# Linear attention gated with a shift-MLP block: DMA transposes, x^T phi(k) in place of v, and the attention output summed into the last MLP product

## The chip, the cores and the metric

The kernel runs on one core of a Trainium2 chip. The metric is the device time of one execution, in microseconds (us). Every number below is a median of several executions, unless one execution is named. The profile is taken of one execution. Its span is from the first to the last instruction. Executions can fall into a slower state, and only runs in the fast state are compared.

TensorE appears in the profile as PE (matmuls) and PEld (weight loads, which overlap matmuls), VectorE as DVE, ScalarE as ACT, GpSimd as POOL, SyncE's queue as SPq. PSUM is the memory that matmuls write to; SBUF is the one that holds their inputs. The granted clock is the share of TensorE's full clock that the throttle let through.

## The reference, cut to what matters

The input x is 2048 tokens by 640 channels. Branch A is linear attention with 32 heads of 20 channels. Branch B is a layernorm, a product with `w1`, a gelu, a shift of token positions, a product with `w2`, then a second layernorm and an MLP of inner width 1728. A gate g per token mixes the two.

```python
g = sigmoid((x * gate_w).sum(-1, keepdims=True))

# branch A; phi(t) = where(t > 0, t + 1, exp(t)) + 1e-6
q, k, v = split(x @ wqkv)                    # 32 heads of 20
kv  = einsum("bhsd,bhse->bhde", phi(k), v)
z   = einsum("bhsd->bhd", phi(k))
num = einsum("bhqd,bhde->bhqe", phi(q), kv)
den = einsum("bhqd,bhd->bhq", phi(q), z)[..., None] + 1e-6
a   = concat_heads(num / den) @ wo

# branch B
h  = gelu(layernorm(x) @ w1)
hs = concat(four quarters of h, shifted by 1, -1, 2, -2 tokens) @ w2
x1 = x + hs
b  = x1 + gelu(layernorm(x1) @ w3) @ w4      # w3: 640 x 1728

out = g * a + (1 - g) * b
```

Two facts let the algebra be rearranged. First, `phi(k)^T v = (x^T phi(k))^T Wv`, so v need never be computed per token. Second, `kv` and `wo` can be multiplied once, to a 640x640 matrix M, so that `a = (phi(q)/den) @ M`. With `g/(1-g) = e^y`, where y is the gate's logit, the output is `(1-g) * (x1 + h2 + (phi(q) * e^y/den) @ M)`, and the last two terms can be accumulated in one PSUM tile.

## The kernel before

The products of this program contract over the partition axis of their inputs, so each activation is needed with channels on partitions. This kernel makes these layouts on TensorE: five 128x128 transposes into PSUM, then one copy by ScalarE.

```python
def transpose_to(dst, src_tok):
    trp = tr_pool["p"].tile([P, DC, P], BF16, name="trp")
    for dc in range(DC):                                   # DC = 5
        nc.tensor.transpose(trp[:, dc, :], src_tok[:, dc * P:(dc + 1) * P], ident[:])
    nc.scalar.copy(dst, trp[:])
```

It is used four times for each of the 16 chunks of 128 tokens: for x, layernorm(x), the attention output o and layernorm(x1). That makes 320 transposes. Outputs of 640 columns are computed in pieces of 512 and 128 columns. The inner width of 1728 is padded with zeros to 14 groups of 128 rows.

```python
if F % P:                                                  # F = 1728, P = 128
    nc.gpsimd.memset(w3_sb[:, :, F:FC * P], 0.0)
    nc.gpsimd.memset(w4_sb[F % P:P, nfull, :], 0.0)
...
# branch A of one chunk, cut
#   pn = phi(q) @ [kv | z];  o_tok = pn * (1/den)
transpose_to(oT[:], o_tok[:])
for (n0, n1) in ((0, 512), (512, D)):
    for dc in range(DC):
        nc.tensor.matmul(pa[:, n0:n1], lhsT=oT[:, dc, :], rhs=wo_sb[:, dc, n0:n1], ...)
nc.scalar.activation(ga[:], pa[:], ACT.Copy, scale=g_all[:, c:c + 1])
...
# last product of one chunk: 28 matmuls
for (n0, n1) in ((0, 512), (512, D)):
    for fc in range(FC):                                   # FC = 14, all of 128 rows
        nc.tensor.matmul(pf[:, n0:n1], lhsT=h2T[:, fc, cc * P:(cc + 1) * P], rhs=w4_sb[:, fc, n0:n1],
                         start=(fc == 0), stop=(fc == FC - 1))
```

Of the kernel before, what the change touches and what calls it, by code (L numbers as in the profile page):

```python
# [8 lines left out]
ACT = mybir.ActivationFunctionType  # L9
# [8 lines left out]
def kernel(  # L18
# [23 lines left out]
    GW = 120  # L42
    NG = 6
    gsz = [GW] * 5 + [D - 5 * GW]
    FC = (F + P - 1) // P
    fsz = [P] * (F // P) + ([F % P] if F % P else [])
    EPS = 1e-5
    CG = D // 4
    shifts = [1, -1, 2, -2]

    x2 = A_x.rearrange("b s d -> (b s) d")
    out2 = out.rearrange("b s d -> (b s) d")

    const = ctx.enter_context(tc.tile_pool(name="const", bufs=1))
    small = ctx.enter_context(tc.tile_pool(name="small", bufs=4))

    ident = const.tile([P, P], BF16)
    make_identity(nc, ident[:])
    hlo = [(P * j) // Dh for j in range(DC)]
    hhi = [(P * j + P - 1) // Dh for j in range(DC)]  # L60
    nhj = [hhi[j] - hlo[j] + 1 for j in range(DC)]
    NHM = max(nhj)
    koff = [0, 160, 320, 512, 672]
    HB0 = 24
    bmask = const.tile([P, DC, NHM * Dh], F32)
    nc.gpsimd.memset(bmask[:], 1.0)
    for j in range(DC):
        off = P * j - Dh * hlo[j]
        nc.gpsimd.affine_select(out=bmask[:, j, :], in_=bmask[:, j, :], compare_op=ALU.is_ge, fill=0.0,
                                base=off, pattern=[[-Dh, NHM], [0, Dh]], channel_multiplier=1)  # L70
        nc.gpsimd.affine_select(out=bmask[:, j, :], in_=bmask[:, j, :], compare_op=ALU.is_ge, fill=0.0,
                                base=Dh - 1 - off, pattern=[[Dh, NHM], [0, Dh]], channel_multiplier=-1)
    ones_col = const.tile([P, 1], BF16)
    nc.vector.memset(ones_col[:], 1.0)

    wo_sb = const.tile([P, DC, D], BF16)
    w2_sb = const.tile([P, DC, D], BF16)
    w3_sb = const.tile([P, DC, FC * P], BF16)
    w4_sb = const.tile([P, FC, D], BF16)
    hsT = const.tile([P, DC, S + 4], BF16)  # L80
    pqT = const.tile([P, DC, S], BF16)
    y_all = const.tile([P, NCH], F32)
    g_all = const.tile([P, NCH], F32)
    omg_all = const.tile([P, NCH], F32)
    kv_ext = const.tile([P, DC, NHM * (Dh + 1)], BF16)
    zc = const.tile([P, DC], F32)

    mid = ctx.enter_context(tc.tile_pool(name="mid", bufs=1))
    w1_sb = mid.tile([P, DC, D], BF16)
    lnxT = mid.tile([P, DC, S], BF16)  # L90
    s1 = ExitStack()
    st1 = s1.enter_context(tc.tile_pool(name="st1", bufs=1))
    wkvg = st1.tile([P, DC, 2 * D + 2], BF16)
    wq_sb = st1.tile([P, DC, D], BF16)
    xT = st1.tile([P, DC, S], BF16)
    x_sb = st1.tile([P, NCH, D], BF16)
    w1p = s1.enter_context(tc.tile_pool(name="w1p", bufs=2))
    ps_tr1 = s1.enter_context(tc.tile_pool(name="ps_tr1", bufs=2, space=PSUM))
    ps_kv = s1.enter_context(tc.tile_pool(name="ps_kv", bufs=1, space=PSUM))
    ps_mm = s1.enter_context(tc.tile_pool(name="ps_mm", bufs=4, space=PSUM))  # L100

    wqkv_v = A_wqkv.rearrange("(c p) f -> p c f", p=P)
    w1_v = B_w1.rearrange("(c p) f -> p c f", p=P)
    nfull = F // P
# [5 lines left out]
    load_x(0, 1)  # L110
    dq.dma_start(wkvg[:, :, 0:512], wqkv_v[:, :, D:D + 512])
    load_x(1, 2)
    dq.dma_start(wkvg[:, :, 512:1024], wqkv_v[:, :, D + 512:D + 1024])
    dq.dma_start(wkvg[:, :, 1024:2 * D], wqkv_v[:, :, D + 1024:3 * D])
    dq.dma_start(wkvg[:, :, 2 * D:2 * D + 1], gate_w.rearrange("(c p o) -> p c o", p=P, o=1))
    load_x(2, 4)
    dq.dma_start(wq_sb[:, :, 0:D], wqkv_v[:, :, 0:D])
    load_x(4, 8)
    for g in range(4):
        dq.dma_start(w1_sb[:, :, P * g:P * (g + 1)], w1_v[:, :, CG * g:CG * g + P])  # L120
        dq.dma_start(w1_sb[:, :, 4 * P + 32 * g:4 * P + 32 * (g + 1)], w1_v[:, :, CG * g + P:CG * (g + 1)])
    load_x(8, 12)
    load_x(12, 16)
    for g in range(4):
        dq.dma_start(w2_sb[:, g, :], B_w2[CG * g:CG * g + P, :])
        dq.dma_start(w2_sb[32 * g:32 * (g + 1), 4, :], B_w2[CG * g + P:CG * (g + 1), :])
    dq.dma_start(wo_sb[:], A_wo.rearrange("(c p) f -> p c f", p=P))
    dq.dma_start(w3_sb[:, :, 0:F], B_w3.rearrange("(c p) f -> p c f", p=P))
    dq.dma_start(w4_sb[:, 0:nfull, :], B_w4[0:nfull * P, :].rearrange("(c p) f -> p c f", p=P))
    if F % P:  # L130
        dq.dma_start(w4_sb[0:F % P, nfull, :], B_w4[nfull * P:F, :])

    if F % P:
        nc.gpsimd.memset(w3_sb[:, :, F:FC * P], 0.0)
        nc.gpsimd.memset(w4_sb[F % P:P, nfull, :], 0.0)
    nc.vector.memset(hsT[:, :, 0:4], 0.0)
    nc.vector.memset(hsT[:, :, S:S + 4], 0.0)
    kvacc = ps_kv.tile([P, 1024], F32)
    nc.vector.memset(kvacc[:], 0.0)
# [13 lines left out]
    def ln_stats(mv_ap, src_ap):  # L153
        st = small.tile([P, 2, 6], F32, name="bnst")
        nc.vector.bn_stats(st[:, 0, :], src_ap[:, 0:D // 2])
        nc.vector.bn_stats(st[:, 1, :], src_ap[:, D // 2:D])
        nc.vector.bn_aggr(mv_ap, st[:])

    tr_pool = {"p": ps_tr1}

    def transpose_to(dst, src_tok):
        trp = tr_pool["p"].tile([P, DC, P], BF16, name="trp")
        for dc in range(DC):
            nc.tensor.transpose(trp[:, dc, :], src_tok[:, dc * P:(dc + 1) * P], ident[:])  # L164
        nc.scalar.copy(dst, trp[:])  # L165

    def phi_from_psum(dst_bf16, src_ps, npart, ncols, tagp):
        e = w1p.tile([P, 640], F32, name="e_" + tagp)
        nc.scalar.activation(e[:npart, :ncols], src_ps, ACT.Exp)  # L169
        nc.vector.tensor_scalar(e[:npart, :ncols], e[:npart, :ncols], 1.0, 1e-6, op0=ALU.min, op1=ALU.add)  # L170
        nc.vector.scalar_tensor_tensor(dst_bf16, src_ps, 0.0, e[:npart, :ncols], op0=ALU.max, op1=ALU.add)  # L171

    xT_done = set()

    def ensure_xT(c):
        if c not in xT_done:
            xT_done.add(c)
            transpose_to(xT[:, :, c * P:(c + 1) * P], x_sb[:, c, :])

    def stage1_chunks(t, ln1_tile=None):  # L180
        if ln1_tile is not None:
            stage1_ln1_stats(ln1_tile)
        for cc in range(CPT):
            c = t * CPT + cc
            cs = slice(c * P, (c + 1) * P)
            xc = x_sb[:, c, :]
            ensure_xT(c)
            if c + 1 < NCH:
                ensure_xT(c + 1)
            pk_sb = w1p.tile([P, D], BF16, name="pk_sb")  # L190
            v_sb = w1p.tile([P, D], BF16, name="v_sb")
            col_blocks = [(0, 512), (512, 1024), (1024, 2 * D + 1)]
            for (c0, c1) in col_blocks:
                pt = ps_mm.tile([P, 512], F32, name="mm")
                for dc in range(DC):
                    nc.tensor.matmul(pt[:, 0:c1 - c0], lhsT=xT[:, dc, cs], rhs=wkvg[:, dc, c0:c1],  # L196
                                     start=(dc == 0), stop=(dc == DC - 1))
                if c0 < D:
                    k1 = min(c1, D)
                    phi_from_psum(pk_sb[:, c0:k1], pt[:, 0:k1 - c0], P, k1 - c0, "k")  # L200
                if c1 > D:
                    v0 = max(c0, D)
                    v1 = min(c1, 2 * D)
                    nc.scalar.copy(v_sb[:, v0 - D:v1 - D], pt[:, v0 - c0:v1 - c0])  # L204
                if c1 > 2 * D:
                    nc.vector.tensor_copy(y_all[:, c:c + 1], pt[:, 2 * D - c0:2 * D - c0 + 1])
            for j in range(DC):
                w_ = Dh * nhj[j]
                v0 = Dh * hlo[j]
                nc.tensor.matmul(kvacc[:, koff[j]:koff[j] + w_], lhsT=pk_sb[:, j * P:(j + 1) * P], rhs=v_sb[:, v0:v0 + w_],  # L210
                                 start=False, stop=(c == NCH - 1), skip_group_check=True)
                nc.tensor.matmul(kvacc[:, koff[j] + w_:koff[j] + w_ + 1], lhsT=pk_sb[:, j * P:(j + 1) * P], rhs=ones_col[:],
                                 start=False, stop=(c == NCH - 1), skip_group_check=True)
            if ln1_tile is not None:
                stage1_ln1_chunk(ln1_tile * CPT + cc)

    ln1_state = {}

    def stage1_ln1_stats(t):
        mv = const.tile([P, CPT, 2], F32, name=f"mv1_{t}")  # L220
        for cc in range(CPT):
            ln_stats(mv[:, cc, :], x_sb[:, t * CPT + cc, :])
        veps = small.tile([P, CPT], F32, name="veps1")
# [14 lines left out]
    def stage1_ln1(t):  # L238
        stage1_ln1_stats(t)
        for cc in range(CPT):  # L240
            stage1_ln1_chunk(t * CPT + cc)
# [262 lines left out]
```

## Time and profile before

The time was 322.37 us (322.27 to 322.65 in four runs). The page's first part gives busy time, share of the span and number of instructions by engine, and its fourth part gives the shares of the chain of work that ended last.

```profile
PE 296.6 (92%) x2064; PEld 160.3 (50%) x2064; DVE 163.7 (51%) x507; ACT 155.7 (48%) x271; POOL 5.5 (2%) x19
...
PE 69%; DVE 13%; ACT 12%; DMA 2%; issue 2%; SPq 1%; ACTq 0%
```

TensorE is busy for 92% of the span and no other engine for more than 51%. So this is a kernel whose time is read from TensorE, and the useful question is how much of the 296.6 us is work and how much is waiting hidden between matmuls. For that I count columns: a matmul streams its columns at 2.4 per ns, plus about 2.5 ns. The traces show this rate: matmuls of 512 and 128 columns follow one another every 216 and 56 ns. The page's groups of instructions show what the work is (line, engine, operation, output<-inputs, shape, count, then busy us and mean ns of one, then idle time before them and its releaser).

```profile
L446 PE MATMUL tokw<-w_sb,h2T 128*128 128x512 bf16 (+1 forms) x392 | 57.5, 299 | 0.6 <-DVE oc L449 0.6
...
L165 ACT COPY xT<-trp 128x640 bf16<-128x640 bf16 x16 | 11.3, 703 | 4.4 <-PE trp L164 4.4
```

The mean of 299 ns in the first of the groups is the length that the profile gives to one matmul, not the distance between two, and it mixes two shapes. Distances between starts are what add up.

| Before, TensorE | columns | us at the stream rate |
|---|---|---|
| k and v projections, gate column | 102,480 | |
| q, w1, w2, o@wo (51,200 each) | 204,800 | |
| w3 and w4 (143,360 each) | 286,720 | |
| phi(k)^T v with z, and phi(q) [kv, z] | about 23,700 | |
| 320 transposes | 40,960 | 17 of the total |
| total | about 658,700 | 279.6 |
| lost: first 20 us / 20 to 100 us / 100 to 175 us / rest | | 14 / 6 / 10 to 12 / the rest of 42 |

The loss between 100 and 175 us is read from the windows: window, its length, then busy us of PE, PEld, DVE, ACT and POOL with instruction counts, the granted clock, the DMA share, GB/s.

```profile
100.00:120.00 20.00, 17.56 (x123) 9.51 (x122) 6.86 (x15) 14.06 (x24) 0.00 (x0) 1.00 0.06 17
...
160.00:180.00 20.00, 16.30 (x125) 8.84 (x123) 15.71 (x49) 6.08 (x8) 0.00 (x0) 1.00 0.11 33
```

### The profile page before, as it was taken

What the parts mean: (1) busy time and instruction counts of PE and PEld (TensorE: products, weight loads), DVE (VectorE), ACT (ScalarE), POOL (GpSimd) and SP (SyncE); (2) the same over time, 40 slices, a digit from 0 to 9 for tenths busy, and PEclk for the clock granted to TensorE, in tenths of its full rate; (3) what the DMA queues carried; (4) which work ended last, traced back from release to release, by engine and by line L of the source; (5) the groups of instructions that cost most, each with busy time, mean ns of one, the idle gap of its engine ahead of it and who ended that gap; (6) DMA issues with size and microseconds to landing.
All of it is one profiled execution on the core that took longest, in us unless ns stands there. A gap on an engine that the chain in (4) does not pass through costs nothing.

```text
span 321.5 us, 5167 instructions
## 1 busy us (share of the span) xinstructions
PE 296.6 (92%) x2064; PEld 160.3 (50%) x2064; DVE 163.7 (51%) x507; ACT 155.7 (48%) x271; POOL 5.5 (2%) x19
## 2 busy tenths in 40 slices
PE   3589999999999799899979899999999999999995
PEld 1246645656544354445435555454555544545453
DVE  4679977585793266423577535960226780111022
ACT  3245656767657936965424442378013368113400
POOL 6000000000000000000000000000000000000000
PEclk9959999999999999999999999999999999999999
DMA  7998930000000011000010011100011000010011
GB/s 237 287 281 270 371 108 1 3 0 2 0 2 0 0 43 43 20 2 0 2 41 20 22 43 41 42 22 0 22 41 43 0 0 3 20 43 21 0 43 41
DMA packets 19144, 17.54 MB, mean 55 GB/s; under 512 B 6768, under 2 KB 18480, under 8 KB 19120
## 3 DMA queue, kind: packets, MB, share of 16 engines
q1 hardware_dynamic: 19120, 17.21, 17.7%
q8 instruction: 16, 0.26, 0.4%
q14 instruction: 8, 0.07, 0.1%
HBM read 14.58 MB, written 2.62 MB: 54 GB/s over the span
## 4 chain that ended last, share of the span: by engine, by line
PE 69%; DVE 13%; ACT 12%; DMA 2%; issue 2%; SPq 1%; ACTq 0%
PE tokw L446 15%; PE mm L196 9%; PE mm L248 6%; PE tokw L330 6%; PE tokc L396 6%; PE trp L164 3%; PE mm L258 3%; PE tokc L446 2%; PE kvacc L210 2%; ACT hsT L266 2%; DMA x_sb<-in_A_x_dram 2%; ACT v_sb L204 2%; PE tokc L373 2%; ACT lnx1T L165 1%; DVE pk_sb L171 1%
## 5 line engine op out<-in xcount | busy, mean ns | idle before, releaser
L446 PE MATMUL tokw<-w_sb,h2T 128*128 128x512 bf16 (+1 forms) x392 | 57.5, 299 | 0.6 <-DVE oc L449 0.6
L196 PE MATMUL mm<-wkvg,xT 128*128 128x512 bf16 (+1 forms) x240 | 51.9, 361 | 3.5 <-DVE pk_sb L171 3.5
L446 PEld LDWEIGHTS <-h2T 128*128 128x128 bf16 x448 | 35.2, 98 | 28.0 <-issue 1.7
L449 DVE SCALAR_TENSOR_TENSOR oc<-tokw,omg_all,ga 128x640 bf16<-128x640 f32 x14 | 12.4, 884 | 71.8 <-PE tokw L446 71.8
L432 PEld LDWEIGHTS <-w_sb 128*128 128x128 bf16 x280 | 25.8, 97 | 25.2 <-issue 1.2
L196 PEld LDWEIGHTS <-xT 128*128 128x128 bf16 x240 | 22.8, 101 | 19.0 <-issue 4.1
L330 PE MATMUL tokw<-w_sb,hsT 128*128 128x512 bf16 (+1 forms) x160 | 27.4, 299 | 4.3 <-ACT hsT L266 1.9
L399 ACT ACTIVATE ga<-tokc,g_all 128x640 f32<-128x640 f32 x16 | 12.7, 791 | 29.4 <-PE tokc L396 29.4
L396 PE MATMUL tokc<-wo_sb,oT 128*128 128x512 bf16 (+1 forms) x160 | 24.7, 300 | 1.4 <-ACT oT L165 1.1
L165 ACT COPY oT<-trp 128x640 bf16<-128x640 bf16 x16 | 11.1, 691 | 28.3 <-PE trp L164 24.6
L248 PE MATMUL mm<-xT,wq_sb 128*128 128x512 bf16 x100 | 22.5, 379 | 0.0
L169 ACT ACTIVATE e_k<-mm 128x512 f32<-128x512 f32 (+1 forms) x32 | 14.0, 437 | 17.5 <-PE mm L196 17.5
L396 PEld LDWEIGHTS <-oT 128*128 128x128 bf16 x160 | 12.4, 98 | 16.9 <-ACT oT L165 7.6
L204 ACT CAST v_sb<-mm 128x256 bf16<-128x256 f32 (+1 forms) x32 | 13.8, 432 | 10.8 <-PE mm L196 5.7
L330 PEld LDWEIGHTS <-hsT 128*128 128x128 bf16 x160 | 13.2, 98 | 11.7 <-issue 3.2
L169 ACT ACTIVATE e_q<-mm 128x512 f32<-128x512 f32 x20 | 11.9, 597 | 10.1 <-PE mm L248 5.2
L170 DVE TENSOR_SCALAR e_k<-e_k 128x512 f32<-128x512 f32 (+1 forms) x32 | 10.2, 319 | 12.8 <-ACT e_k L169 12.6
L171 DVE SCALAR_TENSOR_TENSOR pk_sb<-mm,e_k 128x512 bf16<-128x512 f32 (+1 forms) x32 | 15.5, 485 | 1.1
L258 PEld LDWEIGHTS <-w_sb 128*128 128x128 bf16 x100 | 9.5, 97 | 10.6 <-issue 0.8
L248 PEld LDWEIGHTS <-wq_sb 128*128 128x128 bf16 x100 | 9.5, 98 | 10.4
L171 DVE SCALAR_TENSOR_TENSOR pqT<-mm,e_q 128x512 bf16<-128x512 f32 x20 | 13.8, 688 | 0.4
L165 ACT COPY xT<-trp 128x640 bf16<-128x640 bf16 x16 | 11.3, 703 | 4.4 <-PE trp L164 4.4
(349 smaller groups left out, 438.9 us busy)
## 6 DMA issues: line engine op xcount, KB each, us to landing
xr<-in_A_x_dram SPq DMA_DIRECT2D x16, 160.0 KB, 2.2
out_dram<-oc SPq DMA_DIRECT2D x16, 160.0 KB, 1.8
w_sb<-in_B_w_dram SPq DMA_DIRECT2D x1, 2160.0 KB, 11.9
w_sb<-in_B_w_dram SPq DMA_DIRECT2D x1, 2080.0 KB, 16.6
x_sb<-in_A_x_dram SPq DMA_DIRECT2D x3, 640.0 KB, 7.0
wkvg<-in_A_wqkv_dram SPq DMA_DIRECT2D x2, 640.0 KB, 5.2
w_sb<-in_B_w_dram SPq DMA_DIRECT2D x8, 160.0 KB, 6.1
wq_sb<-in_A_wqkv_dram SPq DMA_DIRECT2D x1, 800.0 KB, 6.8
```

The costliest lines, as they stand in the source:

```text
L165: nc.scalar.copy(dst, trp[:])
L169: nc.scalar.activation(e[:npart, :ncols], src_ps, ACT.Exp)
L171: nc.vector.scalar_tensor_tensor(dst_bf16, src_ps, 0.0, e[:npart, :ncols], op0=ALU.max, op1=ALU.add)
L196: nc.tensor.matmul(pt[:, 0:c1 - c0], lhsT=xT[:, dc, cs], rhs=wkvg[:, dc, c0:c1], start=(dc == 0), stop=(dc == DC - 1))
L204: nc.scalar.copy(v_sb[:, v0 - D:v1 - D], pt[:, v0 - c0:v1 - c0])
L248: nc.tensor.matmul(pt[:, :], lhsT=wq_sb[:, dc, j * P:(j + 1) * P], rhs=xT[:, dc, ts_], start=(dc == 0), stop=(dc == DC - 1))
L258: nc.tensor.matmul(pt[:, :], lhsT=w1_sb[:, dc, fc * P:(fc + 1) * P], rhs=lnxT[:, dc, ts_], start=(dc == 0), stop=(dc == DC - 1))
L330: nc.tensor.matmul(px[:, n0:n1], lhsT=hsT[:, fc, 2 + c * P:2 + (c + 1) * P], rhs=w2_sb[:, fc, n0:n1], start=(fc == 0), stop=(fc == DC - 1))
L396: nc.tensor.matmul(pa[:, n0:n1], lhsT=oT[:, dc, :], rhs=wo_sb[:, dc, n0:n1], start=(dc == 0), stop=(dc == DC - 1))
L399: nc.scalar.activation(ga[:], pa[:], ACT.Copy, scale=g_all[:, c:c + 1])
L432: nc.tensor.matmul(ph[:, :], lhsT=w3_sb[:, dc, fc * P:(fc + 1) * P], rhs=lnx1T[:, dc, :], start=(dc == 0), stop=(dc == DC - 1))
L446: nc.tensor.matmul(pf[:, n0:n1], lhsT=h2T[:, fc, cc * P:(cc + 1) * P], rhs=w4_sb[:, fc, n0:n1], start=(fc == 0), stop=(fc == FC - 1))
```

## The change

The intent: take the transposes off TensorE and ScalarE, replace the v projection by `x^T phi(k)`, fold kv and wo into M, add `phi(q) M` to the last MLP product in the same PSUM tile, pack products with only 32 rows or columns four at a time into the array, and use two halves of 320 columns in place of 512 and 128. The core of the diff, heavily cut (about 830 lines in full; this is nearly a new kernel):

```diff
-load_x(0, 1)
-...
-    nc.tensor.transpose(trp[:, dc, :], src_tok[:, dc * P:(dc + 1) * P], ident[:])
-    nc.scalar.copy(dst, trp[:])
+def load_xT(c0, c1):
+    dq.dma_start_transpose(xT[:, :, c0 * P:c1 * P], x2[c0 * P:c1 * P, :])
+load_xT(0, 1); <k weights, gate column>; load_xT(1, 4); load_xT(4, 8); load_xT(8, 12); load_xT(12, 16)
+...
+nc.sync.dma_start_transpose(lnxT[t][:, :, cc * P:(cc + 1) * P], lnx[:])      # layernorm 1
+nc.sync.dma_start_transpose(lnT[:, :, cc * P:(cc + 1) * P], ln[:])           # layernorm 2
 ...
+def gate_unit():                               # 4 column tiles of 32; z_unit and den_unit alike
+    for dc in range(DC):
+        for t in range(NT):
+            nc.tensor.matmul(pt[32 * t:32 * (t + 1), 0, :], lhsT=gwb[:, dc, :],
+                             rhs=xT[:, dc, t * TS:(t + 1) * TS], ...)
+def g_unit(fc):                                # x^T phi(k)
+    for c in range(NCH):
+        for hf in range(2):
+            nc.tensor.matmul(pt[:, hf, 0:HD], lhsT=x_sb[:, c, fc * P:(fc + 1) * P],
+                             rhs=pk[:, c, hf * HD:(hf + 1) * HD], ...)
+# kv_unit: kvT = gT * wv per head group;  m_unit: M = kvT * wo, groups of 120 rows (and one of 40)
+def scale_unit(j, half):                       # phi(q) *= e^y/den, spread over heads by a 0/1 matrix
+    pts = [pair(), pair()] if half is None else None
+    for part in (r_hi, r_lo):                  # bf16 high and low part of e^y/den
+        for t in range(NT):
+            nc.tensor.matmul(pts[t // 2][:, t % 2, :], lhsT=emat[32 * t:32 * (t + 1), j * P:(j + 1) * P],
+                             rhs=part[32 * t:32 * (t + 1), :], start=(part is r_hi), stop=(part is r_lo))
+    for i in range(2):
+        nc.vector.tensor_tensor(sl, sl, pts[i][:], op=ALU.mult)
 ...
-nc.gpsimd.memset(w3_sb[:, :, F:FC * P], 0.0)
-nc.gpsimd.memset(w4_sb[F % P:P, nfull, :], 0.0)
+FR = F - (FC - 1) * P                          # 64: the last group is no longer padded
+def w4_unit(t, cc):
+    for hf in range(2):                        # 38 matmuls per chunk, 19 per half
+        for j in range(DC):
+            nc.tensor.matmul(pt[:, hf, 0:HD], lhsT=pqT[:, j, c * P:(c + 1) * P],
+                             rhs=m_sb[:, j, hf * HD:(hf + 1) * HD], start=(j == 0), stop=False)
+        for fc in range(FC):
+            w = P if fc < FC - 1 else FR
+            nc.tensor.matmul(pt[:, hf, 0:HD], lhsT=h2[0:w, fc, cc * P:(cc + 1) * P],
+                             rhs=w4_sb[0:w, fc, hf * HD:(hf + 1) * HD], start=False, stop=(fc == FC - 1))
 ...
+# order of the middle stage: w2 of tile 0, layernorm 2 of tile 0, w1 of tile 2,
+for j in range(DC):
+    scale_unit(j, None)                        # all five scaling units in one row
+for fcs in w1_split:
+    w1_unit(3, fcs)                            # last w1 tile
+# then for each tile: w3 (with w2 of the next tile between), layernorm 2 of the next tile, w4
```

## The prediction

> **What bounds the kernel now.** TensorE. The page's busy table gives PE 296.6 us of 321.5 (92%), DVE 51%, ACT 48%. The chain of waits is 69% PE. In its timeline, streams run at full rate: fifteen matmuls of a k/v chunk (6,405 columns) take 2.72 us, five 512-column matmuls 1.08 us, ten of the 512/128 pairs 1.36 us. That is about columns/2.4 ns plus 2.5 ns each. So I count columns: 658,700 in 2,064 matmuls, about 280 us. The other 42 us are losses: about 14 us in the first 20 us (waiting for weights, reduced granted clock), 6 us up to 100 us, 10-12 us between 100 and 175 us (the windows show PE busy 17.6, 18.2, 16.3 of 20; hsT, lnx1T, ga and x1 evacuations), some 4 us later, 2.5 us tail.
>
> **What the change removes.** 320 transposes (40,960 columns, 17 us at the stream rate), their 64 ACT copies (690-700 ns each, 44 us of ACT); the v projection and kvacc, including 80 one-column matmuls; numerator and o@wo (63,300 columns), plus o_tok, rden, ga and u (DVE/ACT).
>
> **What it adds.** x^T phi(k) (51,200, as large as v), kv and M (9,600), phi(q)*M in the last sum (51,200). These trades nearly cancel. Gate, z, denominator and scaling are 112 matmuls of 32 rows or columns, 51,200 columns: 21 us serially. The Trainium skill, "TensorE: Matmul & The Clock Gate", Part 3, Measured speedup vs the span model, gives 3.07x for four row tiles and 2.38x for three column tiles; no run here shows it yet. At about 3x they cost 7 us. Dense work is then 603,600 columns, 255.5 us with per-matmul cost; total PE need about 263 us, against 280.
>
> **What it moves.** Halves of 320 instead of 512/128 save almost nothing: ten matmuls took 1.36 us before, an estimate for ten 320s is the same 1.36; weight loads (97 ns) are already hidden. k evacuation on DVE is about 1.2 us per chunk (estimated from the 640-column 0.88 us and 512-column 0.69 us operations) against 1.36 us of PE, so PE keeps bounding. DVE totals about 160 us as before, but denominators (reciprocal: 32 columns took 350 ns, so 512 columns about 4-5 us) and ten scalings of about 1.2 us cluster between the first w2 tile and the last w1 tile.
>
> **Sum.** PE 263; start 9 (warm-up matmuls, fewer weights before the first k chunk); middle stage 8-10; scattered 5; tail 3: about 290 us, 10% less. All the PE saving is on the critical path.
>
> **Signs.** PE busy about 270-280 us, share 93% or more; no trp groups; w4 chunks of 38 matmuls at about 5.2 us; k chunks every 1.36 us once started; the packed groups start much closer than 213 ns apart; ACT busy near 95-110 us; idle PE mainly before 12 us and around scaling.
>
> **What would make it wrong.** (1) DMA transposes: chunks of 160 KB are consumed every 1.36 us, 120 GB/s. The skill, "DMA: Bandwidth & Descriptors", Latency and other measured facts, gives 261 GB/s effective; this trace has none. At 60 GB/s x alone would take 44 us and the k/q stages lose some 20 us; slow SBUF transposes would also delay w1 and the first w3. (2) Packed matmuls running serially: +14 us. (3) DVE pile-up in the middle: up to +15 us if the instruction order leaves PE behind it (four PSUM pairs only). Each alone still leaves it faster; two together could cancel the gain.
>
> Predicted 290 us, 8 in 10 between 280 and 307; faster 0.90, same 0.06, slower 0.04.

## More of the kernel before

The chain of work that ended last, with start and length in us, has the last product of one chunk as a line of its own:

```profile
302.66 3.80 PE tokw L446 x28
```

These are 28 matmuls in 3.80 us, which is 14 x (216 + 56) ns.

## The result, and the profile after

The time became 301.14 us (300.37 to 302.34 in four runs). The ratio to before is 0.9345, with a 95% interval of 0.931 to 0.9381. Ratios here and below are the mean time of one kernel's fast runs over that of the other's of the same rounds, so they are not quite the ratios of the medians quoted. The outputs were correct.

The same parts of the page after the change, with the row of the TensorE clock from the slices (each digit is one fortieth of the span, the granted clock in tenths):

```profile
PE 286.6 (96%) x1750; PEld 159.5 (53%) x1750; DVE 143.4 (48%) x393; ACT 92.1 (31%) x122; POOL 12.9 (4%) x25
...
PEclk9799999999999995599999999999999999999999
...
PE 76%; DVE 13%; SPq 6%; DMA 2%; issue 1%; ACT 1%; DVEq 0%
```

TensorE did 314 instructions fewer, ScalarE lost 64 us of work, and TensorE is now busy 96% of the span. But the column count says that the dense work is 603,600 columns, 255.5 us, and the packed products about 5.7 us (an estimate for four at a time), together 261.2. So 286.6 us of "busy" hide some 25 us that are not streaming. Two places stand out. The first is the pair of fives in the clock row, at about 112 to 127 us. The second is in the timeline of the last product (start, length, engine, line, operation, shape, count):

```profile
149.31 0.85 PE L454 MATMUL pp<-m_sb,pqT 128*128 128x320 bf16 x5
150.00 2.17 PE L458 MATMUL pp<-w_sb,h_1445 128*128 128x320 bf16 x14
152.09 0.85 PE L454 MATMUL pp<-m_sb,pqT 128*128 128x320 bf16 x5
```

One half of a chunk (5 + 14 matmuls of 320 columns) starts at 149.31 and the next at 152.09: 2.79 us for what is 19 x 136 ns = 2.58 us of streaming. The start times of the single matmuls, worked out from the trace (start in us, distance to the matmul before in ns, rows of the weights), show where the 0.2 us go:

```
151.354  +136  128 rows  w4, group 11
151.489  +135  128
151.625  +136  128
151.857  +232   64 rows  w4, group 14 (the last one, no longer padded)
152.095  +238  128 rows  first of phi(q) M of the next half
152.241  +146  128
152.377  +136  128
```

The matmul that has 64 rows starts 232 ns after its predecessor and the following one 238 ns later. Together with the 146 after them that is 616 ns where three steps of 136 would take 408, and over the whole half the loss is about 200 ns. The weight load of the 64-row matmul is issued at 151.853, 4 ns before its matmul; inside the stream a load is issued about 134 ns ahead of its matmul. At 198 ns each, 32 halves are 6.3 us that the prediction had not foreseen.

The stage with the lowered clock, in the windows (same columns as before):

```profile
79.60:108.80 29.20, 29.10 (x203) 16.14 (x203) 18.23 (x46) 15.10 (x26) 0.00 (x0) 1.00 0.52 121
108.80:120.60 11.80, 7.46 (x42) 1.31 (x42) 11.49 (x22) 5.91 (x9) 0.00 (x0) 0.65 0.28 57
120.60:128.60 8.00, 8.00 (x26) 3.02 (x26) 3.27 (x3) 2.02 (x4) 0.00 (x0) 0.67 0.01 2
```

From 108.8 to 120.6 us the five scaling units run. VectorE is busy 11.49 of 11.80 us, TensorE 7.46. From 120.6 to 128.6 the last w1 tile runs at a clock of 0.67. The chain of work names the cause:

```profile
110.64 1.13 DVE pqT L311
115.95 4.53 DVE pqT L311 x4
120.53 7.11 PE pp L340 x20
```

TensorE's timeline shows its side of it, with the wait and its releaser in brackets:

```profile
111.82 0.39 PE L307 MATMUL pp<-r_hi,emat 32*128 32x512 bf16 x2 [2.01 <-DVE pqT L311]
```

Each scaling unit gives TensorE eight small matmuls and VectorE two multiplications of about 1.2 us each. There is no other work for TensorE in this row of five, so it waits for VectorE. The multiplications are not all that VectorE does there. Its timeline shows that the first one starts only at 110.56 us, 1.8 us after the first scaling matmul (108.78 us), when a row of short operations for the second layernorm has ended:

```profile
110.48 0.16 DVE L420 SCALAR_TENSOR_TENSOR nb_1294<-mv_1206,rstd_1277 128x4 f32<-128x4 f32 x1
110.56 1.21 DVE L311 TENSOR_TENSOR pqT<-pqT,pp 128x1024 bf16<-128x1024 bf16 x1
```

Four multiplications by 1-g, 0.55 us each, also stand between the next ones. So some 3.7 us of the 11.8 are other work in VectorE's order. After the wait of 2.01 us the clock falls to half (from 112.23 to 125.88 us in the trace's record of it): matmuls that took 374 ns take 580 ns from 113.49 us on. The 20 matmuls of the w1 tile then take 7.11 us where 20 steps of 216 ns are 4.3.

The start and the k stage, first in TensorE's timeline, then in VectorE's:

```profile
8.20 0.86 PE L197 MATMUL pp<-wk_sb,xT 128*128 128x321 bf16 x5 [1.11 <-DMA wk_sb<-in_gate_w_dram]
10.08 15.36 PE L197 MATMUL pp<-wk_sb,xT 128*128 128x320 bf16 x100 [1.03 <-DMA xT<-in_A_x_dram]
```

```profile
24.41 0.49 DVE L180 BATCH_NORM_STATS2 bnst<-x_sb 128x6 f32<-128x320 bf16 x1 [1.96 <-DMA x_sb<-in_A_x_dram]
```

Steady work starts at 10.08 us. The 150 matmuls from there to 33.1 us take 23.0 us, where 20.4 are needed: VectorE needs as long per chunk as TensorE (1.37 us, and about 1.46 with layernorm statistics between, against 1.36), stands for 1.96 us in the middle because the next instruction in its order is a layernorm statistic whose input has not landed, and TensorE has only four PSUM pairs (tiles of 2 x 512 columns) to run ahead with. This stage also varies between executions: in the traces of e1 to e4 and e10 below, whose k stage is the same program, it takes 22.4 to 26.6 us.

The packed products and the DMA transposes did what was hoped. First TensorE's timeline of the gate, then two lines of the page's DMA issues (last number: median us from issue to landing):

```profile
43.98 1.26 PE L219 MATMUL pp<-xT,gwb 128*32 128x512 bf16 x20
```

```profile
lnxT<-ln SPq DMA_TRANSPOSE x16, 2.6
xT<-in_A_x_dram SPq DMA_TRANSPOSE x5, 5.7
```

Twenty 512-column matmuls took about 1.3 us. Their starts come in groups of four, 3 to 4 ns apart, and a group starts 227 ns after the first and 216 ns after each later one, the distance of single matmuls. The Trainium skill, "TensorE: Matmul & The Clock Gate", Part 3, Measured speedup vs the span model, states 3.07x for four row tiles and 2.38x for three column tiles; in a stream of groups of four column tiles (the gate) this trace shows close to 4x, and the first two groups of four row tiles (the scaling units) also start 226 ns apart. The DMA transposes of the last fifteen x chunks (2.46 MB) were issued between 3.90 and 17.25 us. If issue limits them, that is about 184 GB/s (an estimate from these two numbers). The skill, "DMA: Bandwidth & Descriptors", Latency and other measured facts, gives 261 GB/s effective. TensorE waited only 1.03 us for them.

The account of the profiled execution, in us of TensorE's span:

| part | predicted | measured |
|---|---|---|
| dense and packed streaming | 263 | 261.2 |
| start | 9 | 8.7 |
| k stage paced by VectorE | 0 | 2.6 |
| middle: 79.6 to 108.8, then scaling and last w1 tile | 8 to 10 | 1.9 + 12.2 |
| 64-row matmuls in the last product | 0 | 6.3 |
| tail, from the end of the last matmul | 3 | 3.6 |
| scattered (the remainder) | 5 | 2.6 |
| span | | 299.1 |
| time of this execution beyond its span | 0 | 2.5 |

The measured column is the streaming estimate and the losses read from the trace in each stretch; the scattered term is what is left.

### The profile page after: what moved, and what is told of

Same layout as the page of the kernel before. It is cut to its first block, busy times and chain, and to the rows that moved or that the text cites. A ratio compares the mean times of both kernels' runs of the same rounds, so it can differ in the third digit from the quotient of the medians.

```text
span 299.1 us, 4325 instructions
## 1 busy us (share of the span) xinstructions
PE 286.6 (96%) x1750; PEld 159.5 (53%) x1750; DVE 143.4 (48%) x393; ACT 92.1 (31%) x122; POOL 12.9 (4%) x25
## 4 chain that ended last, share of the span: by engine, by line
PE 76%; DVE 13%; SPq 6%; DMA 2%; issue 1%; ACT 1%; DVEq 0%
PE pp L458 21%; PE pp L439 20%; PE pp L454 8%; PE pp L246 7%; PE pp L405 6%; PE pp L340 5%; SPq L94 5%; PE pp L208 4%; DVE pqT L311 3%; DVE pk L189 2%; DMA x_sb<-in_A_x_dram 2%; DVE pqT L189 1%; DVE e L188 1%; DVE bnst L180 1%; ACT hsT L352 1%
## 5 line engine op out<-in xcount | busy, mean ns | idle before, releaser
L439 PE MATMUL pp<-lnT,w_sb 128*128 128x512 bf16 (+1 forms) x280 | 63.5, 379 | 0.0
L439 PEld LDWEIGHTS <-w_sb 128*128 128x128 bf16 (+1 forms) x280 | 27.1, 99 | 31.4 <-issue 1.7
L187 ACT ACTIVATE e<-pp 128x640 bf16<-128x640 f32 (+2 forms) x28 | 21.5, 778 | 27.2 <-PE pp L197 19.6
L454 PE MATMUL pp<-m_sb,pqT 128*128 128x320 bf16 x160 | 27.3, 301 | 0.0
L197 PE MATMUL pp<-wk_sb,xT 128*128 128x320 bf16 (+1 forms) x160 | 24.6, 314 | 2.8 <-DMA wk_sb<-in_gate_w_dram 1.1
L405 PE MATMUL pp<-w_sb,hsT 128*128 128x320 bf16 x160 | 23.9, 299 | 0.0
L208 PE MATMUL pp<-xT,wq_sb 128*128 128x512 bf16 x100 | 22.0, 379 | 0.4 <-DVE pqT L189 0.4
L246 PE MATMUL pp<-pk,x_sb 128*128 128x320 bf16 x160 | 21.9, 299 | 0.0
L458 PE MATMUL pp<-w_sb,h_1806 128*128 128x320 bf16 x112 | 17.3, 300 | 0.0
L458 PE MATMUL pp<-w_sb,h_2528 128*128 128x320 bf16 x112 | 17.3, 300 | 0.0
L458 PE MATMUL pp<-w_sb,h_1445 128*128 128x320 bf16 x112 | 17.3, 300 | 0.0
L458 PE MATMUL pp<-w_sb,h_2167 128*128 128x320 bf16 x112 | 17.3, 300 | 0.0
L208 PEld LDWEIGHTS <-wq_sb 128*128 128x128 bf16 x100 | 9.7, 97 | 12.6 <-issue 1.3
L340 PEld LDWEIGHTS <-w_sb 128*128 128x128 bf16 x80 | 8.3, 105 | 11.8 <-issue 4.7
## 6 DMA issues: line engine op xcount, KB each, us to landing
w_sb<-in_B_w_dram SPq DMA_DIRECT2D x1, 800.0 KB, 11.8
```

The source lines that it names most:

```text
L187: nc.scalar.activation(ev, src, ACT.Exp)
L197: nc.tensor.matmul(pt[:, hf, 0:c1 - c0], lhsT=xT[:, dc, cs], rhs=wk_sb[:, dc, c0:c1], start=(dc == 0), stop=(dc == DC - 1))
L208: nc.tensor.matmul(pt[:, i, :], lhsT=wq_sb[:, dc, j * P:(j + 1) * P], rhs=xT[:, dc, ts_], start=(dc == 0), stop=(dc == DC - 1))
L246: nc.tensor.matmul(pt[:, hf, 0:HD], lhsT=x_sb[:, c, fc * P:(fc + 1) * P], rhs=pk[:, c, hf * HD:(hf + 1) * HD], start=(c == 0), stop=(c == ...
L340: nc.tensor.matmul(pt[:, i, :], lhsT=w1_sb[:, dc, CG * fc:CG * fc + P], rhs=lnxT[t][:, dc, :], start=(dc == 0), stop=(dc == DC - 1))
L405: nc.tensor.matmul(pt[:, hf, 0:HD], lhsT=hsT[:, fc, 2 + c * P:2 + (c + 1) * P], rhs=w2_sb[:, fc, hf * HD:(hf + 1) * HD], start=(fc == 0), ...
```

## The experiments

All ratios are to the kernel before, run on the same chip in the same rounds; its median lay between 322.3 and 322.7 us every time. Every kernel gave correct results. Differences from "after" set the median against 301.14 us, which was measured in an earlier session; the kernel before, at the same level in both, ties them.

### e1: pad the last group to 128 rows again

```diff
-    w3_sb = const.tile([P, DC, F], BF16)
+    w3_sb = const.tile([P, DC, FC * P], BF16)
+    nc.gpsimd.memset(w3_sb[:, :, F:FC * P], 0.0)
+    nc.gpsimd.memset(w4_sb[FR:P, FC - 1, :], 0.0)
-            w = P if fc < FC - 1 else FR        # in w3_unit and in w4_unit
+            w = P
```

> The change with the last, 64-row part of w3/w4 padded with zeros to 128 rows, as the kernel before had it. In the changed kernel the 64-row matmul that ends each half of a w4 chunk starts 232 ns after its predecessor and the next 128-row one 238 ns later, where neighbours take 136 ns: 198 ns more per half, 32 halves, 6.3 us, plus about 0.2 us in each of four w3 tiles. Theory (the change of row count breaks the hiding of the weight load): every w4 interval is 136 ns, a half of 19 matmuls takes 2.58 us instead of 2.79, time falls by 6 to 7.5 us to about 294. Rival (what is slow is phi(q)*M joining the sum, or PSUM reads between halves): time within 1 us of the changed kernel.

Measured: 294.80 us (294.53 to 295.36), ratio 0.9150 (0.9121 to 0.9179), 6.3 us less than after. TensorE's timeline of e1 at the same place:

```profile
149.47 0.84 PE L456 MATMUL pp<-m_sb,pqT 128*128 128x320 bf16 x5
150.15 2.06 PE L460 MATMUL pp<-w_sb,h 128*128 128x320 bf16 x14
152.05 0.84 PE L456 MATMUL pp<-m_sb,pqT 128*128 128x320 bf16 x5
```

A half now takes 2.58 us, and all starts are 135 or 136 ns apart. The kernel computes more (64 rows of zeros) and is faster. In the two profiled executions the stretch from the first w4 matmul to the start of the last matmul is 139.5 us, against 145.9 in after: 6.4 us shorter, where 32 x 198 ns are 6.3. That the whole time also differs by 6.3 us is partly luck: e1's k stage took 2.2 us longer and the stretches between it and w4 1.8 us less.

### e2: put the two 64-row matmuls of a chunk side by side

If the cost is that of a 64-row matmul, it comes twice per chunk in any order. If it is that of changing the row count, two neighbours share it.

```diff
+            if hf == 1:                          # second half starts with the 64-row matmul
+                ops = ops[-1:] + ops[:-1]
```

> The change, but the second half of each w4 chunk begins with its 64-row matmul, so the two 64-row matmuls of a chunk are neighbours and there are 16 changes to 64 rows and back instead of 32. Theory (a change of row count costs about 198 ns per there-and-back): 16 x 0.2 = 3.2 us less, about 298. Rival (each 64-row matmul is slow in itself, whatever stands beside it): no change, 301.

Measured: 297.22 us (295.76 to 298.99, six runs), ratio 0.9228 (0.9191 to 0.9265), 3.9 us less than after. In the profiled execution the stretch of the last product is 142.7 us, 3.2 us shorter than in after, as expected; the rest of the difference lies outside it. The starts:

```
150.653  +135  128 rows
150.885  +232   64 rows
151.031  +146   64 rows   (the neighbour)
151.259  +228  128 rows
151.406  +147  128
151.542  +136  128
```

The second 64-row matmul follows after 146 ns, the ordinary distance but for 10 ns. So the cost belongs to each change, about 92 to 102 ns in either direction, and not to the small matmul. What happens inside is not shown by these runs. The trace shows only that the weight load does not run ahead across the change (it is issued 4 ns before its matmul), while its own duration is nearly unchanged (92 ns against 98). The skill, "TensorE: Matmul & The Clock Gate", Part 2, Step-by-step: what each phase is for, says that loads are pulled ahead of matmuls in flight when the row groups do not conflict or the background weight buffer is the target, and that the row count does not matter for a load. For the load's duration the trace agrees; for the overlap it shows a case, the change from 128 to 64 rows and back, in which the load is not pulled ahead.

The row count is not the only change that does this. In after the last w3 group has weights of 128 rows but only 64 columns: the first such matmul starts 309 ns after its predecessor, and the next full one 312 ns after the last of them, where neighbours take 216. Changes from 128 to 32 columns of weights cost about as much (309 against 216 ns at the gate, 229 against 136 at z). So what costs is a change in the shape of the weights, in rows or in columns, and e1 pads away both kinds (w4's rows and w3's columns). Not every change costs: between 120 and 128 columns of weights the starts are the usual 55 and 56 ns apart (e9), while one between 120 and 40 rows costs as much as that to 64 (232 to 243 ns in after). No run has 128 rows next to 120 at the same number of columns.

### e3: put the scaling units between other products

```diff
-    for j in range(DC):
-        scale_unit(j, None)
-    for fcs in w1_split:
+    for j, fcs in enumerate(w1_split):
         w1_unit(3, fcs)
+        scale_unit(j, None)
...
             w3_unit(t, fcs)
+            if t == 0 and i + len(w1_split) < DC:
+                scale_unit(i + len(w1_split), None)
```

> The change with the five scaling units moved from before the last w1 tile into it and into the first w3 tile. Theory (the 11.8 us scaling stretch waits on VectorE's ten 1.2 us multiplications with nothing else for TensorE, and its gaps halve the granted clock for the w1 tile behind it): the gaps and the slow w1 tile go, the time falls by 9 to 13 us to about 290, granted clock over the span 0.99 or so. Rival (scaling is TensorE work that has to be done somewhere): falls by less than 3 us.

Measured: 294.65 us (292.38 to 296.81; the longest run is slow and left out of the ratio), ratio 0.9119 (0.9077 to 0.9161), 6.5 us less than after by medians. The expected size was missed: about 50 to 70% of what was named. The clock (third number from the end of each line) stayed at 1.00 in both stretches, as was to be expected if the halved clock in after came from the idle gaps:

```profile
108.00:120.00 12.00, 9.47 (x59) 3.58 (x57) 9.44 (x28) 9.59 (x16) 0.00 (x0) 1.00 0.44 112
120.00:129.00 9.00, 8.42 (x57) 4.08 (x57) 8.24 (x11) 3.88 (x6) 0.00 (x0) 1.00 0.01 3
```

The first w4 matmul starts at 142.74 us, 6.6 us earlier than in after, so the gain lies in this stage. Part of the wait is left:

```profile
115.39 2.32 PE L340 MATMUL pp<-lnxT,w_sb 128*128 128x512 bf16 x9 [2.48 <-ACT hsT L352]
```

The gelus of the w1 unit before release the PSUM pair late. A scaling unit takes two of the four pairs at once and holds them until VectorE is done, so the units around it have only two.

### e4: leave out the low part

If TensorE's share of the scaling (40 matmuls) was the cost, half of them must show.

```diff
-        for part in (r_hi, r_lo):
+        for part in (r_hi,):
```

> The change without the low part of the scaling factor: 20 instead of 40 scaling matmuls, VectorE unchanged; the result may lose some precision. Theory (VectorE paces the stretch): within 1 us of the changed kernel. Rival (the small matmuls pace it, at 213 ns each one after the other): 4 us faster.

Measured: 300.14 us (297.92 to 300.65, six runs), ratio 0.9295 (0.9261 to 0.9330), 1.0 us less than after by medians, with intervals of the ratios that overlap. In e4's timeline TensorE now simply waits longer before each pair of matmuls:

```profile
117.20 0.61 PE L307 MATMUL pp<-r_hi,emat 32*128 32x512 bf16 x2 [0.59 <-DVE pqT L311]
118.40 0.61 PE L307 MATMUL pp<-r_hi,emat 32*128 32x512 bf16 x2 [0.59 <-DVE pqT L311]
```

The pairs start 1.20 us apart, the length of one VectorE multiplication. The scaling stage is bound by VectorE. In the profiled execution the stretch from the first scaling matmul to the next w1 matmul was 9.8 us, against 11.8 in after. Most of these 2.0 us also come from VectorE's order: its first multiplication starts 0.8 us after the first scaling matmul and not 1.8, and one multiplication by 1-g and not four stands between the first seven. The time does not show the 2.0 us because the k stage of this execution took 3.6 us longer, waiting for VectorE, which itself stood before a load. The timed runs, which varied by 2.7 us, do not let me say more than "about 1 us", so the time alone does not exclude that the small matmuls cost a part.

### e5 and e6: padding and spreading together, then an earlier start

e5 has the padding, one scaling unit after the last w1 tile, and one after each of the first four w3 units; w2 of the next tile moves behind them. e6 adds that the k weights and the gate column are issued from ScalarE's queue and the second transposing load of x is split in two.

```diff
     for fcs in w1_split:
         w1_unit(3, fcs)
+    scale_unit(0, None)
...
+            if t == 0 and i + 1 < DC:
+                scale_unit(i + 1, None)
+            if t == 0 and i >= DC - 1:
+                w2_unit(1, i - DC + 1)
# e6 alone:
-    dq.dma_start(wk_sb[:, :, 0:HD], ...)
+    nc.scalar.dma_start(wk_sb[:, :, 0:HD], ...)      # and the other two pieces
-    load_xT(1, 4)
+    load_xT(1, 2)
+    load_xT(2, 4)
```

> The change with the padding to 128 rows and the scaling units spread over the first w3 tile instead (one after the last w1 tile, four among the w3 units, the next w2 units behind them); the spread of the run before still lost 2.5 us to PSUM held while ScalarE and VectorE finished the second layernorm. If the two losses are independent they add: 6.5 from the padding and 7 to 11 from the spread, 284 to 288 us, with the clock granted in full outside the first 10 us. If the spread only moved the wait on VectorE into w3, it gives under 3 us more than the padding's 294.8.

> The same, with the three loads of the k weights and gate column issued from ScalarE's queue instead of behind the first transposing load on SyncE's, and the second transposing load split so that its first 128 tokens come alone. In the changed kernel the first k chunk waits 1.1 us for the gate column and the second 1.0 us for its transposed x. If those waits are what delays the start, 1 to 2.5 us less than the kernel without it; if the DMA engines' rate is what limits it (their share is full from 10 us on), no difference.

Measured: e5 had a ratio of 0.8957 (0.8894 to 0.902) with fast runs of 286.64, 290.25 and 289.52 us. Its profiled execution took 577.07 us with 512-column matmuls mostly 443 ns apart (559 at times), so its trace is used for nothing. e6: 289.98 us (288.3 to 292.44), ratio 0.9013 (0.8945 to 0.9081). The earlier start bought nothing, and e6's timeline shows why:

```profile
6.99 15.41 PE L199 MATMUL pp<-wk_sb,xT 128*128 128x320 bf16 x100 [1.29 <-DMA xT<-in_A_x_dram]
24.54 9.02 PE L199 MATMUL pp<-wk_sb,xT 128*128 128x320 bf16 x60 [2.14 <-DVE y_all L202]
```

The steady k stream now starts at 6.99 us and not at 10.08, but 2.14 us of that are lost again at 22.4 us, where VectorE stands for 3.55 us before a layernorm statistic whose x has not landed. Here a gain at the start was worth nothing because the next stage's inputs did not come earlier too.

### e7: undo the DMA transposes, each right before its use

```diff
-            nc.sync.dma_start_transpose(lnxT[t][:, :, cc * P:(cc + 1) * P], lnx[:])
+            transpose_to(lnxT[t][:, :, cc * P:(cc + 1) * P], lnx[:])   # TensorE + ScalarE; x and layernorm 2 alike
     for c in range(NCH):
+        transpose_to(xT[:, :, c * P:(c + 1) * P], x_sb[:, c, :])
         k_unit(c)
```

> The change with all DMA transposes undone: x, the first and the second layernorm's output (48 chunks, 240 transposes of 128 columns) go through TensorE and a ScalarE copy again; the second layernorm of the next tile is emitted after the first w4 chunk, or it deadlocks. Theory (transposes were pure TensorE cost on a full engine): 240 x 56 ns = 13.4 us more, plus 1 to 4 us of waits, about 315 to 319. Rival (the gain comes from the algebra and the smaller work of the other engines, and slow transposing loads at the start cost as much as they save): within 4 us of 301.

Measured: 383.06 us (380.91 to 383.18 in the three timed runs), ratio 1.1858; the profiled execution: slow (564 us). This is a failed experiment: it measures a bad placement, not the transposes. In the slow execution, the only one with a trace, every k chunk waits for its own copy, 14.1 us in all:

```profile
14.60 2.46 PE L203 MATMUL pp<-wk_sb,xT 128*128 128x320 bf16 x10 [0.92 <-ACT xT L73]
```

The larger wait in that trace is another one: 35.3 us in which the transposes of the second layernorm wait for ScalarE.

### e8: the kernel before with all its transposes given to the DMA queue

```diff
     def transpose_to(dst, src_tok):
-        ... five nc.tensor.transpose and nc.scalar.copy
+        nc.sync.dma_start_transpose(dst, src_tok)
```

> The kernel before with only this part of the change: its 64 transposes of a chunk go by DMA from SBUF, without PSUM and ScalarE copies. TensorE loses 320 x 56 ns = 17.9 us of work, ScalarE 44 us. Theory (work on the full engine is what counts): 303 to 308 us. Rival (each DMA transpose takes about 2.6 us from issue to landing where TensorE and ScalarE took 1 us, in chains like numerator, o, projection with a single PSUM buffer): the gain is eaten, 315 us or more.

Measured: 357.68 us (356.2 to 358.47), ratio 1.1088 (1.1042 to 1.1134): 35 us slower than before, although TensorE's busy time fell to 279.2 us. The queue of SyncE in e8 shows the reason:

```profile
25.99 7.05 SPq L131 DMA_DIRECT2D w_sb<-in_B_w_dram  x1
33.08 16.60 SPq L162 DMA_TRANSPOSE xT<-x_sb  x10
```

The transposes of x, which need x in SBUF first, stand in program order behind the weight loads (the last `w4` load holds the queue from 25.99 to 33.04 us). The first is issued at 33.08 and the first matmul runs at 41.58 us. TensorE also waits 7.1 us in 13 places for the transposed attention output, as the rival said. Again this measures placement.

### e9 and e12: the same two questions, placed well

e9 is after with all transposes on TensorE, but each chunk's transposes are emitted one or more units ahead of their use. e12 is before with x transposed by DMA straight from DRAM, first in the queue as in after, and both layernorms by DMA; only o keeps its TensorE transposes, as it is made and used within one chunk.

```diff
# e9, against after
+    xT_tr(0)
+    xT_tr(1)
     for c in range(NCH):
+        xT_tr(c + 2)
         k_unit(c)
# ... layernorm chunks between g, kv, w1, w2, scaling and w4 units
# e12, against before
-    load_x(0, 1)
+    load_xT(0, 1)                       # and the other x chunks, before wq and x_sb
-        transpose_to(lnxT[:, :, cs], lnx[:])
+        transpose_to(lnxT[:, :, cs], lnx[:], dma=True)        # lnx1T alike; oT stays
```

> The undoing of all DMA transposes again, now placed as the kernel before placed its own: the transposes of x two chunks ahead of their use, those of the first layernorm between other TensorE units, those of the second between scaling units and w4 chunks. The first try lost 0.9 us of idle TensorE in every k chunk to the ScalarE copy it waited for, which is a fault of placing and not a price of the transposes. Theory (240 transposes of 56 ns on a full engine): 13.4 us and up to 5 us of waits more than the changed kernel, 314 to 320. Rival (transposes cost mainly by the waits they put into TensorE's order): 325 or more even so. Rival (they were filled into idle time): within 4 us of 301.

> The kernel before with DMA transposes placed as the change places them: x comes transposed from DRAM in five loads ahead of the other loads, both layernorms go by DMA from SBUF, the attention output stays on TensorE (its chain of waits made the first try of this part slow, and so did transposes queued behind 25 loads until 33 us). If the DMA transposes alone carry the gain, as the version of the change without them (325.5) suggests: 300 to 307. If they need the rest of the change (PSUM in pairs, no o transposes, work to hide the landing time): 312 to 325.

Measured: e9 325.51 us (323.11 to 327.39), ratio 1.0092 (1.0015 to 1.0170). e12 306.15 us (305.82 to 307.43), ratio 0.9487 (0.9457 to 0.9517). Their engine lines, e9 then e12:

```profile
PE 304.3 (94%) x1976; PEld 175.8 (54%) x1990; DVE 145.7 (45%) x393; ACT 122.3 (38%) x170; POOL 13.2 (4%) x27
```

```profile
PE 278.9 (91%) x1790; PEld 146.2 (48%) x1824; DVE 160.0 (52%) x507; ACT 127.3 (42%) x223; POOL 5.5 (2%) x19
```

Without the DMA transposes the change is not faster than before at all; with them alone, before gains 16.2 of the 21.2 us. In e12's profiled execution TensorE's busy time is 17.7 us shorter than before (296.6 to 278.9; the 240 transposes are 13.4 of it, the rest is not assigned) and its idle time 1.9 us longer. The gain is not one of the new start alone: the first w1 matmul comes 5.7 us earlier, the first w3 matmul 8.4, the last w3 matmul 15.9. Of the 24.4 us between e9 and after, 240 transposes at 56 ns are 13.4 us. Most of the rest are waits: TensorE is idle for 19.9 us in e9 and 12.6 in after. e9's view of TensorE's waits (us in total, times, longest) names the largest:

```profile
PE pp L72 <- ACT ln L451: 5.9, 6, 1.6
PE pp L72 <- DMA x_sb<-in_A_x_dram: 3.1, 1, 3.1
```

A TensorE transpose needs its input at its place in TensorE's order, so a late layernorm stops everything behind it; a DMA transpose moves that wait to SyncE's queue. e9's 24.4 us is an upper bound for the price, as a still better order might hide some of these waits.

### e10: the padded version with 512 and 128 columns in place of two halves of 320

```diff
-        for hf in range(2):                       # in w2_unit and w4_unit of e1
+        for (n0, n1) in ((0, 512), (512, D)):
```

> The padded version with w2 and the last product in pieces of 512 and 128 columns, as before the change, instead of halves of 320. Theory (weight loads are hidden in both forms, the rate is columns/2.4 ns plus 2.5 ns): 38 matmuls of a w4 chunk take 5.17 us in both, time within 1 us of the padded 294.8. Rival (a 97 ns weight load does not fit under a 56 ns matmul of 128 columns, which is why the change went to halves): 41 ns more for each of 384 matmuls of 128 columns, 15 us slower.

Measured: 293.13 us (293.06 to 294.22), ratio 0.9105 (0.9065 to 0.9146), against 294.80 and 0.9150 of e1. The intervals overlap. The starts are 216 ns apart for nineteen matmuls and 56 ns for nineteen, which is 272 ns for a pair of pieces, as 2 x 136 is for a pair of halves. Halves of 320 save nothing.

### e11: padding, an earlier start, and scaling units only between w3 units

```diff
     for fcs in w1_split:
         w1_unit(3, fcs)
+    w2_unit(1, 0)
+    w2_unit(1, 1)
     for t in range(NT):
         for i, fcs in enumerate(w3_split):
             w3_unit(t, fcs)
+            if t == 0 and i < DC:
+                scale_unit(i, None)
+            if t == 0 and i >= DC:
+                w2_unit(1, i - DC + 2)
# with e1's padding and e6's start; x chunks 0 to 3 loaded ahead of wq
```

> Padding, loads of the k weights from ScalarE's queue, the first four chunks of x loaded before the q weights, and two of the next w2 units put between the last w1 tile and the first w3 tile, with the five scaling units after the first five w3 units. In the run with the second spread TensorE waited 1.9 us for the transposed second layernorm and 1.2 us for a PSUM pair before it, at half clock for 1.4 us after, and 2.1 us in the k stage because VectorE stood at a layernorm operation whose x had not landed. If these are the waits left: 4 to 6 us less than the 289.9, about 284 to 286. If the x loads only trade places with the q weights: about 288.

Measured: 285.94 us (285.2 to 286.41), ratio 0.8872 (0.8833 to 0.8911). This is the fastest kernel, 15.2 us under after and 36.7 us under before by medians. In e11's timeline the first w4 matmul starts 9.1 us earlier than in after, and of the middle stage one wait over 1 us is left:

```profile
119.11 2.32 PE L442 MATMUL pp<-lnT,w_sb 128*128 128x512 bf16 x9 [1.01 <-DMA lnT<-ln]
...
140.17 0.84 PE L457 MATMUL pp<-m_sb,pqT 128*128 128x320 bf16 x5
```

The waits of the k stage stayed (2.2 us for transposed x, and 2.5 us for VectorE, which stood 4.09 us before x): loading the first x chunks ahead of wq did not cure it.

## Why the prediction was right or wrong

**Right: what bounds the kernel, and that the saving lies on the critical path.** The prediction said that TensorE bounds it and that the removed work shortens it directly. e12 shows this from one side (transposes by DMA alone: 16.2 us less) and e9 from the other (transposes back on TensorE: 24.4 us more). The two numbers differ, so the effects are not simply additive. The part of the transposes themselves, 240 x 56 ns, is 13.4 us in both.

**Right: packed products cost little.** Gate, z and denominator took 1.26, 1.20 and 1.20 us of TensorE, since a stream of groups reaches nearly 4x and not the 3x taken from the skill. With the scaling units at the same rate (an estimate, as these waited for VectorE) that is under 6 us, where the prediction had 7.

**Right: the DMA transposes keep up, and halves of 320 save nothing.** TensorE waited 1.03 us for xT, and e10 gave the same time as e1 within the intervals. Risks (1) and (2) of the prediction did not occur.

**Wrong by 6.3 us: "w4 chunks of 38 matmuls at about 5.2 us".** They took 5.58 us. The sum costed every matmul by its columns alone, as the before kernel's stream had shown, but in that kernel all of these had 128 rows. The diff drops the zero padding, and the prediction gave this no cost. Padding (e1) takes the 6.3 us away, and e2 shows that they belong to the changes between 128 and 64 rows and not to the small matmuls.

**Mis-sized: "middle stage 8-10".** It measured 14.1 us (1.9 + 12.2). The prediction named VectorE's ten multiplications of about 1.2 us and listed the pile-up as risk (3), so the mechanism was right. What it left out was the layernorm work that stands before and between these multiplications on VectorE (some 3.7 us), that the clock falls after the wait, and that the following w1 tile pays for that too (7.11 us for 4.3). The prediction's risk came true in part. e3 and e11 take most of it away by order alone; in e4, with half the small matmuls, TensorE simply waits longer, so VectorE sets the pace.

**Wrong by 2.6 us: "so PE keeps bounding" in the k stage.** The estimate of 1.2 us of VectorE work per chunk, against 1.36 of TensorE, was too low: with the gate column's copy it was 1.37 us and with layernorm statistics between about 1.46, and one stand before a late load reaches through four PSUM pairs.

**Left out: 2.5 us between span and time.** The sum added up a span and called it the time. The page before showed the gap already (321.5 against 322.4 to 322.7).

**Offsets.** Streaming was 1.8 us cheaper, scattered losses 2.4 us smaller. Added up from the predicted sum: 289 + 6.3 + 4.9 (middle against 9.2) + 2.6 + 2.5 - 1.8 - 2.4 + 0.6 (tail) - 0.3 (start) is 301.4, against 301.63 measured in this execution. The sum has to close, since the scattered term is the remainder. So the interval held the result, and the point missed by 11 us for reasons that nearly all lay in details of the new program's order and shapes, not in its algebra.

**The sign "PE busy about 270-280 us"** was missed too (286.6), for the same reasons: time lost to changes of shape and to a halved clock counts as busy in the profile (TensorE is busy 8.00 of 8.00 us in the window with the clock at 0.67).

**What stays open.** The part of the algebra (x^T phi(k), M, the joint sum) has no run of its own. Its columns nearly cancel: about 617,700 without transposes before, against 603,600 and 51,200 packed ones that cost as 12,800. Between e12 and after lie 5.0 us; the 80 o transposes at 56 ns, which after no longer has, are 4.5 us of TensorE work. How much the algebra is worth is not shown, as the same program also carries the losses that e1 and e3 remove. Why a change of shape stops the load from running ahead is not shown. And two profiled executions (e5's, e7's) ran at about half rate; their cause was not looked into.

## What to carry to other kernels

In a stream of matmuls keep the shape of the weights constant and pad with zeros if need be: here each half that ended in 64 rows cost 198 ns, and with the zeros every matmul took its usual 135 or 136 ns. When a stage gives another engine more work than TensorE, do not emit its units in a row; put unrelated matmuls between them; here the clock fell to half otherwise and the stage after paid as well. Look also at what else stands in the other engine's order. Transposes by DMA are worth three quarters of this change, but only where they stand early in their queue and their result has time to land: the same replacement, for the attention output too and behind 25 weight loads, made the kernel 11% slower.

## What the Trainium skill lacked or had wrong

- "TensorE: Matmul & The Clock Gate", Part 2, Step-by-step: it says that the row count does not matter for the time of a weight load. The load's duration agrees (92 ns for 64 rows, 98 ns for 128), but at a change from 128 to 64 rows and back, matmul starts are 232 and 238 ns apart and not 136, a loss of 198 ns per half; two 64-row matmuls side by side are 146 ns apart. A change from 128 to 64 columns of weights and back costs as much (309 and 312 ns for 216). This page has no such case; "TensorEngine Tiling (Array Packing)", Key Properties, says that a change of tiling mode drains TensorE, but gives no time for it. Whether these changes are such changes of mode is not shown.
- The same page, Part 3, Measured speedup vs the span model: 3.07x for four row tiles, 2.38x for three column tiles. In a stream of groups of four column tiles, this trace shows group starts 216 to 227 ns apart with 3 to 4 ns inside a group, so close to 4x.
- The same page, Part 1, HAM oscillation: how this bites in real kernels, gives as its rule that TensorE should have no idle gap over about 3.4 us. Here the clock was halved (from 112.23 to 125.88 us) though the longest wait of TensorE was 2.01 us; in e3, with a wait of 2.48 us, it stayed at 1.00. So the longest single gap did not decide it here; what did is not shown.
- "DMA: Bandwidth & Descriptors", Latency and other measured facts: 261 GB/s effective for a DMA transpose. The x loads here were issued at about 184 GB/s (an estimate from 2.46 MB in 13.35 us of queue time), with weight loads beside them, so this run does not test the page's figure. The page gives no latency for one transpose within SBUF: 160 KB landed in 2.6 us (median).
- No page that I found has a whole execution at about half rate: e7's profiled execution took 564 us with a mean clock of 0.552, and e5's took 577 us, with 512-column matmuls mostly 443 ns apart. The 1.000 that is listed as e5's clock says nothing, as its trace holds no record of the clock.
